# Attention and an FFN in one kernel: the first K in two loads, V of the first head group earlier, and the sums of the first batch loosened from its value passes

## The chip, the cores and the metric

The kernel runs on one core of one Trainium2 chip. The metric is the device time of one execution in microseconds (us); the median of several runs is compared. A difference is stated against the kernel before on the same chip.

Five engines work side by side, each through its own instructions in order: TensorE (PE in the profile; its weight loads are PEld), VectorE (DVE), ScalarE (ACT), GpSimd (POOL, which here only issues the loads) and SyncE (SP, which issues the stores). They wait for each other by semaphores.

## The reference, cut to what matters

```python
def _attn_ref(q, k, v):                     # each (8, 12, 448, 64): batch, heads, tokens, dim
    scale = 1.0 / np.sqrt(q.shape[-1])
    scores = scale * np.matmul(q, k.transpose(0, 1, 3, 2))
    scores = scores - np.max(scores, axis=-1, keepdims=True)
    attn = np.exp(scores)
    attn = attn / (np.sum(attn, axis=-1, keepdims=True) + 1e-09)
    return np.matmul(attn, v)

def _moe_ref(x, w_in, w_out):               # x (3584, 768), w_in (768, 2048), w_out (2048, 768)
    h = x @ w_in
    g = h * (1.0 / (1.0 + np.exp(-h)))
    return g @ w_out
```

The heads of a token are laid side by side (12 x 64 = 768) between the two. Inputs and the output are float32.

## The kernel before, in words

**Data.** Loads convert to float16 on the way. A *head group* is four of the twelve heads of a batch, so a batch has three groups. In a group's tile for K or Q, partition 32h + i holds head h and the fourteen tokens 14i to 14i + 13. VectorE transposes it in 32x32 blocks, so that the head dimension comes onto partitions: `turn_k` (line 371) and `turn_q` (line 392). Since two float16 values are moved as one float32, a score is made of two products (even and odd dims, `e` in `score`, line 398). The key tokens of K are put in four chunks `c` of up to 128 keys: token `first + c` of each of four sets `x` (`X_TOK`, line 234). For the first group ("lone") the sets begin at tokens 0, 4, 8 and 12, and the last has two tokens only, so that chunks 0 and 1 have 128 keys and chunks 2 and 3 have 96 (`KROWS`).

**Stages.** For each group: scores (line 403), exponentials from PSUM into SBUF (`expo`, line 434), the sums of the exponentials by a product with ones (`attend`, part 0; line 494 for batch 0, line 480 for pairs of groups later), two value passes (`attend`, parts 1 and 2; line 465), and the division: `inverse` (line 533) turns the sums (539), inverts them (556) and spreads the inverses over the tokens (560), and `norm` (line 593) multiplies. Then the FFN: the first product (609), tanh (625) and gate (650), and the second product, in plain form for the first 256 rows (`plain`, line 830; line 832) and with seven products in place of eight for the rest (line 820). The last four batches make the first product in the same manner (line 740).

Batch 0 is cut into two pieces of queries (seven and seven token sets), so its three groups make six *units*, numbered 0 to 5: units 0 to 2 are the first queries of groups 0 to 2, units 3 to 5 the second. In batch 0 two chunks of scores lie in one burst (`per_burst`). Units 0 to 3 (`TILED = 4`) write scores into three pairs of PSUM banks (`s_ring`), while sums and values share two banks (`m_ring`).

**The order.** Nothing is ordered at run time. A planner (`Order`, line 96, and the loop at line 1735) plays the kernel through with estimated times, and writes each engine's instructions in the order in which it started them. Its constants (such as `DMA_ROW`, `NEAR`, `HOLD`, `SHY`) are estimates and preferences; they cost nothing on the chip, but change the order. An operation starts in the plan when `when(deps)` has passed: a dependency is an operation, or a pair of it and a slack which is taken off its end. VectorE and ScalarE take the ready operation with the lowest time plus `bias`.

- `Order.load` (157) prices a load by rows and bytes. The POOL queue issues loads in the order of their planning (lines 946 to 982): K and Q of groups 0, 1, 2, then V of the whole batch in four loads, then further Q, w_in in four quarters of three loads, K and Q of batch 1, w_out in four quarters, V of batch 1 between its second and third quarter, then batch by batch.
- `qk_at` and `run_qk` start scores, `av_at` (1598) and `run_av` start sums and value passes. These stand in one list, `av_seq`: sums, values 1, values 2 of unit 0, then of unit 1, and so on. Only its first is looked at.
- `after_sums` (1673) plans the three steps of the inverse. The first waits for the inverse of the unit before (`inv_op[-1:]`), the last also for the last four norms (`norm_op[-4:]`), since the spread inverses of all units lie in the same place, `R[:, 0]`.
- `moe` is the list of FFN work, from which `moe_ready` (1438) takes the first that is ready. `queue_ffn1` (1018) puts in the first product, whose `deps` name the w_in loads; `queue_plain` (1268) puts in the plain second product, in steps of four with the w_out loads.
- Where PE would wait before the first FFN product, `run_zeros` (1719) multiplies zeros into an idle bank. The first stretch of it has `FIRST` blocks of 128 columns.

Of the kernel before, what the change touches and what calls it, by code (L numbers as in the profile page):

```python
# [9 lines left out]
FP16 = mybir.dt.float16  # L10
# [9 lines left out]
DMA_ROW = 0.022  # L20
DMA_RATE = 13400.0
DMA_SLOW = 13
DMA_GAP = 1.1
# [72 lines left out]
class Order:  # L96
# [60 lines left out]
    def load(self, rows, row_bytes, emit, ring=None, gate=None):  # L157
        op = Op("POOL", 0.58, emit)
        self.loads += 1
        row = DMA_ROW if self.loads <= DMA_SLOW else 0.004  # L160
        took = rows * (row + row_bytes / DMA_RATE) / 16 + DMA_GAP * (self.loads == 3)
        self.pool.append((op, took, ring, gate))
        return op
# [50 lines left out]
def kernel(  # L214
# [14 lines left out]
    HG = 4  # L229
# [21 lines left out]
    NEAR = 0.05  # L251
    LATE = -1.0
    COLD, FIRST = 8.5, 47
# [5 lines left out]
    COPY_B = -1  # L259
# [3 lines left out]
    HOLD = 0.4  # L263
    TILED = 4
    QUART = 1
    TURN = 4
    LOOK = 1
# [3 lines left out]
    SHY = 0.8  # L271
    TWB = 4
    SXB = 8
    PIECES = ((0, 7), (7, TPP))
# [36 lines left out]
    sT_t, inv_t, q_tile = {}, {}, {}  # L311
# [5 lines left out]
    def load_k(b, hg):  # L317
        t = sb.tile([128, TPP * D], FP16, name=f"rk_{b}_{hg}", tag="rk", bufs=NRK)
        nc.gpsimd.dma_start(out=t, in_=group_of(k, b, hg))
        rawk[(b, hg)] = t  # L320
# [50 lines left out]
    def turn_k(b, hg):  # L371
        t = rawk[(b, hg)][:].bitcast(FP32).rearrange("p (g i) -> p g i", i=32)
        kt = sb.tile([128, NCH, 4, 32, 2], FP16, name=f"KT_{b}_{hg}", tag="KT", bufs=3)
        KT[(b, hg)] = kt
        pairs = kt.rearrange("p c x i e -> p (c x i e)").bitcast(FP32)
        pairs = pairs.rearrange("p (c x i) -> p x c i", c=NCH, x=4)
        toks = X_TOK[form(b, hg)]
        x = 0
# [154 lines left out]
    def inverse(ns, step):  # L533
# [23 lines left out]
        else:  # L557
            for i, n in enumerate(ns):
                rdn_t[n] = R[:, i, 0 : g1 - g0]
            nc.vector.transpose(  # L560
                out=R[:, 0 : len(ns), 0 : g1 - g0],
# [355 lines left out]

    def plan_q(n):
# [15 lines left out]
    def plan_w_in(f0, f1):  # L934
        made = [
            od.load(256, 2 * (f1 - f0), lambda c=c: load_w_in(c, f0, f1))
# [10 lines left out]
    for hg in range(NG):  # L947
        plan_k(0, hg)
        plan_q(hg)
    plan_v(0, 0, NG)  # L950
# [33 lines left out]
    turned = {"n": 0}  # L984
# [30 lines left out]
    inv_op, norm_op = [], []  # L1015
    quads = []

    def queue_ffn1(b, g0, g1):
# [6 lines left out]
        for fs in turns:  # L1025
# [41 lines left out]
            def deps(fs=fs):  # L1067
                made = [(x_op[(b, cc, g0)], cc * mm(t1 - t0)) for cc in range(NDC)]
                made += [x for f in fs for x in ld_win[f]]
# [198 lines left out]
    def queue_plain(t, j):  # L1268
# [8 lines left out]
        def queue(f0, f1):  # L1277
# [16 lines left out]
            def deps():  # L1294
                if len(parts) < f0 // NPL:
                    return [None]
                made = [ld_wout[i] for i in range(len(ld_wout)) if wout_rows[i] < f1]
# [183 lines left out]
    def qk_at():  # L1481
# [10 lines left out]
        at = when([kt_op.get(units[n][:2]) for n in ns] + [qt_op.get(n) for n in ns])  # L1492
# [7 lines left out]
    def run_qk():  # L1500
# [4 lines left out]
        if n < TILED:  # L1505
            tiles = dict(zip(ys, s_ring.take(len(ys))))
# [91 lines left out]
    def av_at():  # L1598
        if not av_seq:
            return None  # L1600
        ns, part = av_seq[0]
# [71 lines left out]
    def after_sums(ns, op, nq, bank):  # L1673
        folds = per_burst(ns[0])
        last = norm_op[-4:]
# [156 lines left out]
```

## Time and profile before

| what | us | where from |
|---|---|---|
| median of three runs (388.13 to 388.76) | 388.36 | runs |
| profiled execution | 388.74 | run |
| its span, first to last instruction | 386.9 | page |
| first K issued, landed | 1.24, 4.87 | POOL timeline, time to landing |
| first Q landed | 5.40 | the same |
| second K and Q landed | 7.91, 8.50 | the same |
| third K and Q landed | 9.63, 10.22 | the same |
| V of batch 0 landed, four loads | 11.19, 12.19, 13.24, 13.77 | the same |
| w_in quarters landed | 18.43, 23.63, 29.76, 33.48 | the same |
| w_out quarters landed | 39.53, 43.62, 56.25, 60.06 | the same |
| first score on PE | 5.95 | PE timeline |
| first exponential | 6.56 | ACT timeline |
| first value pass | 16.00 | PE timeline |
| first FFN product | 24.70 | PE timeline |
| end of the last product | 383.1 | PE timeline |

All times count from the start of the span. A landing is the time of issue and the time to landing of that issue. In a row of the profile, `E<-P` names what is written and what is read, then the shape; in brackets stands how long the engine was idle before it, and what ended that.

### The profile page before, as it was taken

What the parts mean: (1) busy time and instruction counts of PE and PEld (TensorE: products, weight loads), DVE (VectorE), ACT (ScalarE), POOL (GpSimd) and SP (SyncE); (2) the same over time, 40 slices, a digit from 0 to 9 for tenths busy, and PEclk for the clock granted to TensorE, in tenths of its full rate; (3) what the DMA queues carried; (4) which work ended last, traced back from release to release, by engine and by line L of the source; (5) the groups of instructions that cost most, each with busy time, mean ns of one, the idle gap of its engine ahead of it and who ended that gap; (6) DMA issues with size and microseconds to landing.
All of it is one profiled execution on the core that took longest, in us unless ns stands there. A gap on an engine that the chain in (4) does not pass through costs nothing.

```text
span 386.9 us, 9007 instructions
## 1 busy us (share of the span) xinstructions
PE 378.5 (98%) x3569; PEld 191.1 (49%) x3569; DVE 297.5 (77%) x549; ACT 245.1 (63%) x381; POOL 87.9 (23%) x159
## 2 busy tenths in 40 slices
PE   8999998999999999999999999999999999999996
PEld 4567753443344444344434345555556655555653
DVE  2477676988988888898878879978887747777662
ACT  4979885798977677887568885316772038872000
POOL 7663453604224516060325000000000000000000
PEclk9999999999999999999999999999999999999999
DMA  7999999933719586483595200131001340001333
GB/s 113 200 206 208 179 167 210 164 60 35 110 31 180 88 154 87 59 108 59 105 167 72 43 2 20 29 87 31 0 2 41 100 107 0 2 0 44 102 93 92
DMA packets 37210, 34.41 MB, mean 89 GB/s; under 512 B 11696, under 2 KB 37168, under 8 KB 37168
## 3 DMA queue, kind: packets, MB, share of 16 engines
q0 software_dynamic: 26416, 22.82, 39.9%
q1 hardware_dynamic: 9984, 10.24, 9.7%
q10 hardware_dynamic: 768, 0.79, 0.8%
q8 instruction: 28, 0.46, 0.5%
q14 instruction: 14, 0.11, 0.1%
HBM read 45.61 MB, written 11.01 MB: 146 GB/s over the span
## 4 chain that ended last, share of the span: by engine, by line
PE 86%; DMA 9%; DVE 1%; POOL 1%; issue 1%; ACT 0%; ACTq 0%; DVEq 0%; POOLq 0%
PE P L820 29%; PE P L740 16%; PE P L609 16%; PE P L403 9%; PE P L465 9%; DMA rq<-in_q_dram 4%; DMA w_out_t<-in_moe_w_out_dram 3%; PE P L832 2%; DMA rk<-in_k_dram 2%; PE P L480 2%; PE P L1721 1%; POOL V L349 1%; PE P L494 1%; DVE ost L872 0%; DMA out_dram<-ost 0%
## 5 line engine op out<-in xcount | busy, mean ns | idle before, releaser
L439 ACT ACTIVATE E<-P 128x448 f16<-128x448 f32 (+4 forms) x172 | 151.9, 918 | 45.1 <-PE P L403 44.1
L609 PE MATMUL P<-xT,w_in_t 128*128 128x448 f16 (+1 forms) x480 | 81.4, 316 | 0.0
L349 POOL DMA_DIRECT2D V<-in_v_dram x84 | 46.0, 566 | 94.6 <-PE P L465 68.5
L609 PEld LDWEIGHTS <-w_in_t 128*128 128x128 f16 x480 | 43.0, 98 | 36.8 <-issue 16.0
L820 PEld LDWEIGHTS <-G 128*128 128x128 f16 x400 | 38.1, 98 | 29.3 <-issue 5.0
L403 PE MATMUL P<-rq,KT 32*128 32x448 f16 (+4 forms) x864 | 50.4, 340 | 0.4 <-ACT E L439 0.3
L650 DVE SCALAR_TENSOR_TENSOR G<-G,P 128x448 f16<-128x448 f16 x64 | 38.5, 609 | 13.3 <-ACT G L625 12.6
L820 PEld LDWEIGHTS <-S 128*128 128x128 f16 x312 | 29.6, 98 | 24.1 <-issue 4.9
L820 PE MATMUL P<-w_out_t,S 128*128 128x384 f16 x208 | 39.1, 326 | 0.7 <-DVE ost L872 0.7
L820 PE MATMUL P<-D,G 128*128 128x384 f16 x208 | 38.9, 326 | 0.0
L597 DVE SCALAR_TENSOR_TENSOR xT<-P,R 128x448 f16<-128x448 f32 (+1 forms) x54 | 28.4, 565 | 11.9 <-PE P L465 10.6
L625 ACT ACTIVATE G<-P 128x448 f16<-128x448 f32 x64 | 34.5, 545 | 3.4 <-PE P L609 2.7
L872 DVE TENSOR_TENSOR ost<-P,u 128x384 f32<-128x384 f32 x39 | 21.6, 554 | 18.2 <-PE P L820 13.9
L820 PE MATMUL P<-w_out_t,G 128*128 128x384 f16 x192 | 34.9, 326 | 0.0
L465 PE MATMUL P<-E,V 128*32 128x448 f16 (+2 forms) x672 | 34.3, 355 | 0.0
L740 PE MATMUL P<-sx,tw 128*128 128x448 f16 x144 | 30.2, 352 | 0.0
L740 PEld LDWEIGHTS <-tw 128*128 128x128 f16 x192 | 18.8, 98 | 17.5
L403 PEld LDWEIGHTS <-KT 32*128 32x128 f16 (+2 forms) x864 | 14.2, 98 | 26.4 <-issue 24.3
L879 ACT COPY ost<-P 128x384 f32<-128x384 f32 x13 | 6.3, 484 | 32.8 <-PE P L820 27.5
L384 DVE STREAM_TRANSPOSE KT<-rk 128x256 f32<-128x256 f32 (+3 forms) x48 | 16.6, 385 | 10.1 <-DMA rk<-in_k_dram 10.1
L465 PEld LDWEIGHTS <-V 128*32 128x32 f16 (+2 forms) x672 | 13.8, 95 | 20.0 <-issue 13.2
L450 DVE TENSOR_TENSOR T<-T,E 128x1792 f16<-128x1792 f16 x20 | 21.6, 1081 | 0.1
(78 smaller groups left out, 447.2 us busy)
## 6 DMA issues: line engine op xcount, KB each, us to landing
out_dram<-ost SPq DMA_DIRECT2D x208, 48.0 KB, 1.6
rk<-in_k_dram POOLq DMA_DIRECT2D x24, 224.0 KB, 5.4
rq<-in_q_dram POOLq DMA_DIRECT2D x21, 224.0 KB, 5.8
w_in_t<-in_moe_w_in_dram POOLq DMA_DIRECT2D x12, 256.0 KB, 8.4
w_out_t<-in_moe_w_out_dram POOLq DMA_DIRECT2D x4, 768.0 KB, 11.5
V<-in_v_dram POOLq DMA_DIRECT2D x43, 64.0 KB, 4.0
V<-in_v_dram POOLq DMA_DIRECT2D x40, 48.0 KB, 4.1
out_dram<-ost ACTq DMA_DIRECT2D x16, 48.0 KB, 1.8
```

The lines of the kernel that those rows point to most:

```text
L349: nc.gpsimd.dma_start(out=VT[(b, hg0)][32 * x : 32 * (x + 1), :, 0:count, :], in_=v[b, hs].rearrange("h (i g) d -> i h g d", g=TPP)[:, :, ...
L403: nc.tensor.matmul(out=P[p0 : p0 + 32 * (x1 - x0), pS[h], at : at + nq], lhsT=KT[(b, hg)][32 * h : 32 * (h + 1), c, x0:x1, :, e], rhs=QT[n ...
L439: nc.scalar.activation(out=E[(n, w)][0:kr, h0:h1, 0:nk], in_=P[0:kr, bank : bank + h1 - h0, 0:nk], func=AF.Exp, scale=attn_scale,)
L450: nc.vector.tensor_tensor(out=T[n], in0=T[n] if step else E[(n, 0)], in1=E[(n, step + 1)], op=ALU.add,)
L465: nc.tensor.matmul(out=a[32 * h : 32 * (h + 1), 0:nq], lhsT=w, rhs=e[k0:k1, h, at : at + nq], start=start, stop=stop, skip_group_check=True,)
L597: nc.vector.scalar_tensor_tensor(out=xc(b, cc)[:, 32 * g0 : 32 * g1], in0=acc[(n, part)][:, 0:nq], scalar=0.5, in1=rdn_t[n].rearrange("p g ...
L609: nc.tensor.matmul(out=h_t[(b, f, t0)][:, 0 : t1 - t0], lhsT=w_in_t[:, cc, 128 * f : 128 * (f + 1)], rhs=xc(b, cc)[:, t0:t1], start=(cc == 0),
L625: nc.scalar.activation(out=g, in_=h, func=AF.Tanh)
L650: nc.vector.scalar_tensor_tensor(out=g, in0=g, scalar=1.0, in1=h, op0=ALU.add, op1=ALU.mult)
L740: nc.tensor.matmul(out=pp_t[(*key, PBANK[m])], lhsT=w[:, c, :], rhs=xc(pb + x[0], 3 * x[1] + c) if isinstance(x, tuple) else sx_t[(pb, x)] ...
L820: nc.tensor.matmul(out=pr_t[(qd, BANK[m])][:, 0:OH], lhsT=w[:, f, :], rhs=W_[m][:, f, :], start=(f == 0 and BANK[m] == m), stop=(f == HF - 1),
L872: nc.vector.tensor_tensor(out=out, in0=a, in1=b, op=op)
```

## The change

Four things, and a number of the planner's constants:

- The first K comes in two loads, and the first Q ahead of both (`plan_first`). Part 0 has the token pairs 0, 2, 4 and 6 (eight tokens), which are chunks 0 and 1; part 1 the pairs 1, 3 and 5, which are chunks 2 and 3. Each part has its own turn, and the scores of chunk 0 ask only for the first.
- V of batch 0 comes in two sets of four loads: group 0 alone, ahead of K and Q of group 2 (`VFIRST = 2`), and groups 1 and 2 after them.
- In batch 0 the spread inverses get a buffer of four slots, `rdn_0`, in one of the two T buffers. The spreading waits for the norms of the unit that had the slot before, four units back. `av_at` may take the next sums of batch 0 ahead of the first in the list if that isn't ready.
- Prices of loads are changed (`DMA_ROW`, `DMA_GAPS`), w_out loads count as landed 1.3 us later (`SURE`) and w_in loads 0.39 us later, and `NEAR`, `FIRST`, `COPY_B`, `HOLD`, `LOOK` and `SHY` have other values.

```diff
-DMA_ROW = 0.022
+DMA_ROW = 0.004
-DMA_SLOW = 13
-DMA_GAP = 1.1
+DMA_GAPS = {1: 0.3, 3: 0.7, 4: 0.7}
...
-        row = DMA_ROW if self.loads <= DMA_SLOW else 0.004
-        took = rows * (row + row_bytes / DMA_RATE) / 16 + DMA_GAP * (self.loads == 3)
+        took = rows * (DMA_ROW + row_bytes / DMA_RATE) / 16 + DMA_GAPS.get(self.loads, more)
...
-    NEAR = 0.05
+    NEAR = 0.25
-    COLD, FIRST = 8.5, 47
+    COLD = 8.5
+    FIRST = 41
-    COPY_B = -1
+    COPY_B = -4
-    HOLD = 0.4
+    HOLD = 0.2
+    VFIRST = 2
-    LOOK = 1
+    LOOK = 2
-    SHY = 0.8
+    SHY = 1.0
+    SURE = -1.3
...
+    def load_k(b, hg, part=None):
+        if (b, hg) not in rawk:
+            rawk[(b, hg)] = sb.tile(
+                [128, TPP * D], FP16, name=f"rk_{b}_{hg}", tag="rk", bufs=NRK
+            )
+        t, src = rawk[(b, hg)], group_of(k, b, hg)
+        if part is not None:
+            t, src = token_pairs(t)[:, part::2], token_pairs(src)[:, part::2]
+        nc.gpsimd.dma_start(out=t, in_=src)
+
+    def token_pairs(t):
+        return t.rearrange("p (y e) -> p y e", y=TPP // 2)
...
+        if part is not None:
+            t = t.rearrange("p (y c) i -> p y c i", c=2)[:, part::2]
+            nc.vector.transpose(
+                out=pairs[:, 0 : 4 - part, 2 * part : 2 * part + 2], in_=t
+            )
+            return
...
+            homes = R[:, 0 : len(ns), 0 : g1 - g0]
+            if per_burst(ns[0]) == 2:
+                if "t" not in rdn_0:
+                    rdn_0["t"] = sb.tile([128, HG, S], FP16, name="rdn_0", tag="T", bufs=NT_)
+                at = ns[0] % HG
+                homes = rdn_0["t"][:, at : at + 1, :].rearrange("p h s -> p (h s)").bitcast(FP32)
+                homes = homes.rearrange("p (n g i) -> p n g i", n=1, i=32)
             for i, n in enumerate(ns):
-                rdn_t[n] = R[:, i, 0 : g1 - g0]
+                rdn_t[n] = homes[:, i]
             nc.vector.transpose(
-                out=R[:, 0 : len(ns), 0 : g1 - g0],
+                out=homes,
...
+    def plan_first():
+        plan_q(0)
+        made = [
+            od.load(512 - 128 * i, 4 * D, lambda i=i: load_k(0, 0, i), None if i else rk_ring)
+            for i in range(2)
+        ]
+        kt_ring.take()
+        turns = [
+            Op("DVE", 0.155 + (8 - 2 * i) / 30.0, lambda i=i: turn_k(0, 0, i), [made[i]], TURN,
+               then=rk_ring.give if i else None)
+            for i in range(2)
+        ]
+        kt_first.append(turns[0])
+        kt_op[(0, 0)] = turns[1]
...
     for hg in range(NG):
+        if hg == VFIRST:
+            plan_v(0, 0, 1)
+        if hg == 0:
+            plan_first()
+            continue
         plan_k(0, hg)
         plan_q(hg)
-    plan_v(0, 0, NG)
+    plan_v(0, int(VFIRST < NG), NG)
...
-                made += [x for f in fs for x in ld_win[f]]
+                made += [(x, 0.3 * SURE) for f in fs for x in ld_win[f]]
...
-                made = [ld_wout[i] for i in range(len(ld_wout)) if wout_rows[i] < f1]
+                made = [(ld_wout[i], SURE) for i in range(len(ld_wout)) if wout_rows[i] < f1]
...
+        made = [kt_op.get(units[n][:2]) for n in ns] + [qt_op.get(n) for n in ns]
+        if n == 0 and c == 0:
+            made[0] = kt_first[0]
...
-            tiles = dict(zip(ys, s_ring.take(len(ys))))
+            tiles = s_ring.take(len(ys))
+            if qk_seq[0][0][0] >= TILED:
+                tiles.sort()
+            tiles = dict(zip(ys, tiles))
...
-        ns, part = av_seq[0]
+        at = part_at(*av_seq[0])
+        if units[av_seq[0][0][0]][0] or (at is not None and at <= od.now):
+            return at
+        for i, (ns, part) in enumerate(av_seq[:12]):
+            if i and part == 0 and units[ns[0]][0] == 0:
+                first = part_at(ns, part)
+                if first is not None and (at is None or first < at):
+                    at = first
+                    av_seq.insert(0, av_seq.pop(i))
+                break
+        return at
...
+        if folds == 2:
+            if not rdn_op:
+                t_ring.take()
+            last = norm_ops.get(ns[0] - HG, [])
```

## The prediction

> **What bounds the kernel now.** I read the page first, then the chain of waits, then the first 62 us by engine. The page's slices say that TensorE is the bound:
>
> ```profile
> PE 378.5 (98%) x3569; PEld 191.1 (49%) x3569; DVE 297.5 (77%) x549; ACT 245.1 (63%) x381; POOL 87.9 (23%) x159
> ...
> PE   8999998999999999999999999999999999999996
> ```
>
> But busy is not work: line 1721 multiplies zeros to keep the array going. The windows of that line alone (columns: stretch, length, PE busy and matmuls, PEld, clock, DMA share, GB/s):
>
> ```profile
> 0.00:6.00 6.00, 4.63 (x12) 1.60 (x12) 1.00 0.59 79
> 6.00:10.00 4.00, 1.89 (x10) 0.80 (x10) 1.00 1.14 172
> 10.00:16.00 6.00, 4.20 (x26) 1.94 (x25) 1.00 1.38 199
> 16.00:20.00 4.00, 0.41 (x3) 0.10 (x1) 1.00 1.25 203
> 20.00:25.00 5.00, 0.23 (x1) 0.10 (x1) 1.00 1.20 207
> ```
>
> That is 11.35 us. In the same 25 us all PE rows are busy 22.53 us (4.68+3.71+6.00+4.00+4.14), so only 11.2 of the first 25 us are work; 13.8 us are zeros or nothing. From the first FFN product at 24.70 to the end of the last at 383.1 its gaps are 1.36, 0.70 and 0.11 us (at 60.1, 198.3 and 286.3). A change to the start can win only there, and must then keep it.
>
> Who ends the waits in the start? The timeline, ACT and PE rows:
>
> ```profile
> 6.56 10.35 ACT L439 ACTIVATE E<-P 128x896 f16<-128x896 f32 x12 [4.54 <-PE P L403]
> 17.11 1.73 ACT L439 ACTIVATE E<-P 128x896 f16<-128x896 f32 x2 [0.21 <-PE P L403]
> 19.30 1.72 ACT L439 ACTIVATE E<-P 96x896 f16<-96x896 f32 x2 [0.46 <-PE P L403]
> 22.27 1.72 ACT L439 ACTIVATE E<-P 128x1344 f16<-128x1344 f32 x2 [1.25 <-PE P L403]
> 24.81 1.29 ACT L439 ACTIVATE E<-P 96x1344 f16<-96x1344 f32 x1 [0.81 <-PE P L403]
> ```
> ```profile
> 16.00 0.57 PE L465 MATMUL P<-E,G 128*32 128x224 f16 x16
> ...
> 23.88 0.35 PE L465 MATMUL P<-E,G 96*32 96x224 f16 x5 [0.86 <-issue]
> 24.16 0.61 PE L403 MATMUL P<-rq,KT 32*96 32x224 f16 x16
> 24.70 1.80 PE L609 MATMUL P<-xT,w_in_t 128*128 128x224 f16 x17
> ```
>
> Until 16.9 the exponentials run without a gap (12 in 10.35, 0.863 us each): ACT is the bound and PE fills. Then ACT begins to wait for scores, because the value passes of line 465, none before 16.00, come all at once with sums, norms and the scores. DVE is busy 4.79 of the 5 us from 20 to 25. The first FFN matmul is at 24.70.
>
> The last view is who PE waits for in the whole span:
>
> ```profile
> PE P L832 <- DMA w_out_t<-in_moe_w_out_dram: 1.4, 1, 1.4
> PE P L1721 <- DVE cols L294: 1.2, 1, 1.2
> PE P L465 <- issue: 0.9, 1, 0.9
> PE P L820 <- DVE ost L872: 0.7, 1, 0.7
> PE P L403 <- ACT E L439: 0.3, 1, 0.3
> ```
>
> The first row is at 58.74 to 60.10: the fourth quarter of w_out lands at 60.06 (issued 49.34, 10.72 to landing). It is a clock that does not depend on PE.
>
> **First K in two loads.** Before, K lands at 4.87 (224 KB), Q at 5.40 (336 KB together), two turns take 0.70, the Q turn 0.37, the first score is at 5.95. After, Q (112 KB) and eight of the K's fourteen tokens (128 KB) suffice: 240 KB. Between the two landings 112 KB took 0.53, so 240 KB are there at 4.95. The Q turn (0.37) lies before that. A turn of 256 elements takes 0.43 (its row in the first 62 us), and the first score followed the turn by 0.05: 5.43 or, with a semaphore's slack, 5.46. **Gain 0.49**; bounds 0.04 (it lands only at 5.40) and 0.6 (lands at 4.87). The eleven zero matmuls that FIRST = 41 leaves (one less at 0.43) end by then. Issuing costs one more POOL step, 0.57, before the second K; that load is queued anyway (issued 2.46, landed 7.91). The second turn (192 elements, 0.34) lies behind the first scores and their 0.86 us of exponential; if these came late, it would cost its 0.34.
>
> The K loads become 896 rows of 256 B in SBUF. The nearest row is the last V load of the first batch, 384 rows of 256 B, 96 KB: it landed 0.53 after the one ahead of it (13.77 against 13.24), 181 KB/us, against 192 KB in 1.05 us for 512 B rows. So 224 KB cost 1.24 instead of some 1.13 us: 0.1 later for all behind. I keep 0.1 to 0.3.
> By the Trainium skill (DMA: Bandwidth & Descriptors, "Why small descriptors are slow (HBM only)") a 256 B descriptor loses 3 of 11 bus cycles, which as an estimate would make it 0.34 us and the total 0.2 us worse; the V row is nearer to the smaller loss, and decides.
>
> **V of head group 0 ahead of the third K.** Four more issues (0.54 to 0.69 each), and 224 KB are moved ahead of K and Q of group 2. Landings in order of bytes, taken from the landings before: 896 KB at 9.63, so V of group 0 at 9.7; K of group 2 at 10.8 (was 9.63), Q at 11.4 (was 10.22), the rest of V at 13.9, where all of V was at 13.77. POOL: at each time eight loads are out (the eleventh was issued at 8.19, after the third landed at 7.91); with the smaller ones that is still over 500 KB, 2.6 us at 195 KB/us, against 2.2 us from issue to landing in an empty queue (V loads at 45.9 to 47), so the transfers don't run dry. Group 2 now has K and Q turned at 11.8 (0.70 and 0.37; the K turn is done before the Q lands). Its scores are wanted at 12.74 - 0.49 = 12.25. It fits by 0.4; if it failed, ACT would idle for the difference. The same holds of a value pass that PE meets before its V has landed: scores stand behind it in PE's order, and ACT waits for them. The planner counts V as 1.0 later than its own estimate, which covers it.
>
> **Sums and inverses.** The sums passes (8 matmuls, 0.40 apart from the next) no longer stand behind value passes, and each group's inverse has a slot of its own, so it need not wait for the norms of the group before. Before, sums of groups 1, 2, 3 run at 17.41, 19.59, 21.16; they can now run as soon as their exponentials end, at about 13 and 16.5. No instruction is added; the slots lie in one of the two T buffers, free since the first add into T is at 47.92 and the last norm of batch 0 at 34.62. The inverse chain (0.65+0.17+0.20+0.41) moves from DVE's full stretch at 20 to 25 into 10 to 16, where it is busy 41%.
>
> **The sum for the start.** Real work done at 24.70 is 10.9 us. After: exponentials of four groups end at 6.07 + 16 x 0.863 = 19.9 (before 21.02). By 19.1, when the first w_in quarter is due (landed 18.43, plus 0.1, plus the new 0.4 of caution), PE can have done scores of four groups (8 x 0.51), sums of three (1.2) and values of three (3.0): 8.3 us. From there 24 FFN matmuls (2.2 us) and group 3's values are at hand and PE is full: 10.9 is reached at 21.7. The 0.86 "issue" wait agrees as a limit: adding up the counts it stands before the 349th matmul (23.88), and the 221st was at 18.46, 5.4 us earlier; if 128 matmuls can't come faster than that, the 349th can be at about 10.9 + 10.8 = 21.7 at the soonest (the 93rd, at 11.26 before, by 10.9). So at most 3.0 us; every link without a gap. **I take 2.3 us** (it contains the 0.49), nearer to the upper bound, since ACT, PE and DVE each have free time in 13 to 20; bounds 0.5 (the early first score alone) and 3.3.
>
> **The w_out wait.** PE would be at its place by 56.4, and the fourth quarter lands at 60.1 to 60.4. The plain products are planned as in `queue_plain`, whose loads now count as 1.3 us later, so others go first. At hand are the first twelve steps of the second and third plain tile, which need three quarters (third landed 56.25): 24 x 0.163 = 3.9 us, and sums and values of the head pair (0.7 + 3.1, run at 62.14 to 68.5 before). Banks and the exponentials of the pair decide. Bounds: -2.3 (all given back) to +1.4 (also the old wait gone). **I take +0.4.** Batch 2's scores stay where they are (its Q lands at 62.20, turned 63.26, scores 63.58); PE has the FFN of batch 1 instead.
>
> **The other constants** (NEAR, HOLD, LOOK, SHY, COPY_B) change the written order up to 250 us. Past the w_out wait PE's gaps there are one of 0.7 us, which bounds the gain; the loss by the gaps that another order can open, two of that size: -1.5. I take -0.2.
>
> Sum: 2.3 + 0.4 - 0.2 = 2.5. The profiled execution was 388.74 in all (span 386.9 and 1.84 around it), the median 388.36; 2.5 off gives 386.2 and **385.9**. Its own range is 384.5 to 387.1.
>
> **Rivals.**
> 1. *w_out takes it all back.* The wait grows from 1.4 to 3.7 us and PE leaves it at 60.1 to 60.4 as before. For: the landing is fixed by a queue that runs from 1.24 on. Against: the 3.9 us of plain steps named. Time 388.4. Chance 0.13.
> 2. *Group 2 comes late*, by the four V issues and loads now ahead of its K: ACT idles 0.5 to 1 us, and values move less. Or the planner leaves the values late, so that the change hardly does what it says. Gain 1.0: 387.4. Chance 0.14.
> 3. *Slower: copies ahead of exponentials.* COPY_B from -1 to -4 lets the two PSUM copies of each of 13 quads (0.48 each, 12.5 us) go ahead of exponentials, on whose banks the scores wait; ACT is 74% busy from 100 to 150 and 76% from 150 to 200. PE waits only if nothing else is ready. To be slower than before by 0.2% it needs 3.3 us, a quarter of the 12.5. At a third, 4.1 us: 390.0. Against: PE had other work at nearly each such time. Chance 0.11.
>
> **Chances.** Forecast 0.62, rivals 0.13, 0.14, 0.11. A difference of 0.2% (0.78 us) is about what can be told from none. Faster: 0.62 + 0.09 of rival 2 + 0.03 of rival 1 = 0.74; same 0.05 + 0.07 = 0.12; slower 0.11 + 0.03 = 0.14. The range, with the upper bound of the start (3.3 + 1.4) below and rival 1 above, is 383.9 to 388.6.
>
> **What would show it.** First score at 5.4 to 5.6; first value pass at 10 to 12; zeros (line 1721) down from 11.35 to 7 to 9 us; first FFN matmul at 18.5 to 21; exponentials gapless to 20; the L832 wait under 1 us. It is wrong if the fourth w_out quarter still ends a wait of 2 us or more, or if new gaps of PE stand between 100 and 250.

## The result, and the profile after

The changed kernel is slower: 393.78 us median of four runs (392.41 to 396.09) against 388.56 (388.13 to 389.71) on the same chip. The ratio is given as 1.0119 with a 95% interval of [1.0075, 1.0162]; the quotient of the two medians alone is 1.0134. The profiled execution took 392.41, its span 390.6.

The page, busy time and the 40 slices (PEclk is the granted clock in tenths):

```profile
PE 379.4 (97%) x3561; PEld 190.7 (49%) x3561; DVE 298.0 (76%) x549; ACT 245.0 (63%) x381; POOL 90.9 (23%) x164
...
PE   6999997999999999999989999999999999999996
...
PEclk8799999999999999999999999999999999999999
```

TensorE is busy 0.9 us longer with eight instructions fewer, and its clock is below full in the first two slices, which it wasn't before. The zeros, the same windows as before (line 1721 has become 1802; columns: stretch, length, PE busy, PEld busy, clock, DMA share, GB/s):

```profile
0.00:6.00 6.00, 3.78 (x12) 1.43 (x12) 1.00 0.65 69
6.00:10.00 4.00, 0.73 (x2) 0.21 (x2) 0.67 1.17 158
10.00:16.00 6.00, 2.92 (x11) 1.02 (x12) 0.65 1.20 156
16.00:20.00 4.00, 1.60 (x10) 0.51 (x7) 1.00 1.12 166
20.00:25.00 5.00, 1.42 (x8) 0.65 (x8) 1.00 1.23 203
```

10.45 us of zeros where there were 11.35, so little is won; the clock is 0.67 and 0.65 where it was 1.00; and the loads move 156 and 166 GB/s from 10 to 20 us where they moved 199 and 203. The ACT timeline, and the PE rows that answer to the two of before:

```profile
7.65 3.39 ACT L456 ACTIVATE E<-P 128x896 f16<-128x896 f32 x4 [5.63 <-PE P L420]
12.53 1.73 ACT L456 ACTIVATE E<-P 128x896 f16<-128x896 f32 x2 [1.49 <-PE P L420]
15.31 10.13 ACT L456 ACTIVATE E<-P 96x896 f16<-96x896 f32 x11 [1.05 <-PE P L420]
```
```profile
6.98 0.69 PE L420 MATMUL P<-rq,KT 32*128 32x224 f16 x16 [2.00 <-DVE KT L391]
...
14.16 0.57 PE L482 MATMUL P<-E,G 128*32 128x224 f16 x16
...
24.04 1.32 PE L633 MATMUL P<-xT,w_in_t 128*128 128x224 f16 x12
```

The first exponential is 1.09 us later, ACT then waits twice for scores, the first value pass is 1.8 us sooner, and the first FFN product 0.7 us. Who PE waits for in the whole span:

```profile
PE P L420 <- DVE rq L412: 2.0, 1, 2.0
PE P L420 <- DVE KT L391: 2.0, 1, 2.0
PE P L1802 <- DVE cols L295: 1.2, 1, 1.2
PE P L844 <- DVE ost L896: 1.2, 1, 1.2
PE P L482 <- DVE G L674: 0.8, 1, 0.8
```

The wait for w_out's fourth quarter (1.4 us before) is gone. Two of 2.0 us have come: for the first K, and for a turned Q at 65.8, which is batch 2's.

**Loads**, each from its issue and its time to landing, us:

| | before | after |
|---|---|---|
| first Q | 5.40 | 4.25 |
| first K (its two parts after) | 4.87 | 5.53 and 6.37 |
| V of group 0 complete | 13.77 | 10.62 |
| third K, third Q | 9.63, 10.22 | 11.71, 12.34 |
| V of batch 0 complete | 13.77 | 15.49 |
| first, second w_in quarter | 18.43, 23.63 | 21.72, 26.69 |
| fourth w_out quarter | 60.06 | 62.91 |
| first K and Q of batch 2 | 61.15, 62.20 | 63.97, 65.09 |

**Work done.** To compare runs I count PE's products without the zeros, by their columns (those that fill only a 32-row or 32-column strip at a quarter), scaled so that 346.8 us are the whole. What a kernel has done at a time can then be set beside the kernel before:

| at, us | before | after | difference |
|---|---|---|---|
| 16 | 2.68 | 2.68 | 0 |
| 28 | 11.49 | 9.57 | -1.9 |
| 60 | 38.66 | 38.01 | -0.7 |
| 66 | 44.00 | 41.37 | -2.6 |
| 240 | 204.25 | 200.65 | -3.6 |

1.9 us are lost by 28, most of it is made good by 60 (the kernel before waits for w_out there), and 2 us are lost again at 60 to 66. The rest is lost in small pieces. The end is 3.7 us later.

### The profile page after: what moved, and what is told of

Same layout as the page of the kernel before. It is cut to its first block, busy times and chain, and to the rows that moved or that the text cites. A ratio compares the mean times of both kernels' runs of the same rounds, so it can differ in the third digit from the quotient of the medians.

```text
span 390.6 us, 8992 instructions
## 1 busy us (share of the span) xinstructions
PE 379.4 (97%) x3561; PEld 190.7 (49%) x3561; DVE 298.0 (76%) x549; ACT 245.0 (63%) x381; POOL 90.9 (23%) x164
## 4 chain that ended last, share of the span: by engine, by line
PE 85%; DMA 9%; POOL 2%; issue 1%; DVE 1%; ACT 1%; SPq 0%; DVEq 0%; POOLq 0%; ACTq 0%
PE P L844 29%; PE P L764 16%; PE P L633 15%; PE P L420 10%; PE P L482 9%; DMA rq<-in_q_dram 7%; DMA rk<-in_k_dram 2%; PE P L856 2%; PE P L497 2%; PE P L1802 2%; POOL V L358 1%; PE P L511 1%; ACT E L456 1%; DVE ost L896 0%; DMA out_dram<-ost 0%
## 5 line engine op out<-in xcount | busy, mean ns | idle before, releaser
L420 PE MATMUL P<-rq,KT 32*128 32x448 f16 (+4 forms) x864 | 51.8, 345 | 4.0 <-DVE rq L412 2.0
L621 DVE SCALAR_TENSOR_TENSOR xT<-P,R 128x448 f16<-128x448 f32 x42 | 24.3, 617 | 7.5 <-PE P L482 6.1
L482 PEld LDWEIGHTS <-V 128*32 128x32 f16 (+2 forms) x672 | 13.9, 95 | 20.2 <-issue 13.4
## 6 DMA issues: line engine op xcount, KB each, us to landing
w_out_t<-in_moe_w_out_dram POOLq DMA_DIRECT2D x4, 768.0 KB, 11.4
```

Source lines behind the costliest of these rows:

```text
L420: nc.tensor.matmul(out=P[p0 : p0 + 32 * (x1 - x0), pS[h], at : at + nq], lhsT=KT[(b, hg)][32 * h : 32 * (h + 1), c, x0:x1, :, e], rhs=QT[n ...
L482: nc.tensor.matmul(out=a[32 * h : 32 * (h + 1), 0:nq], lhsT=w, rhs=e[k0:k1, h, at : at + nq], start=start, stop=stop, skip_group_check=True,)
L621: nc.vector.scalar_tensor_tensor(out=xc(b, cc)[:, 32 * g0 : 32 * g1], in0=acc[(n, part)][:, 0:nq], scalar=0.5, in1=rdn_t[n].rearrange("p g ...
```

## The experiments

Ratios are against the kernel before on the same chip and occasion, where its median was 389.56 to 390.04; they stand with a 95% interval, and are not the quotients of the medians.

### One part of the change undone

**e1_one_k**: the changed kernel with the first K in one load, ahead of the first Q.

```diff
-DMA_GAPS = {1: 0.3, 3: 0.7, 4: 0.7}
+DMA_GAPS = {3: 1.1}
-    FIRST = 41
+    FIRST = 47
-        if hg == 0:
-            plan_first()
-            continue
```

> The K split undone alone (K of group 0 in one load ahead of its Q, FIRST 47, gap 1.1 at the third load as before); V first, sums and the other constants stay. Theory A (the split is the cause: the first turn waits for both parts, 6.37, PE idles 2.0 us and the array's clock falls; 256 B rows slow the queue): first score at 5.95, no wait of PE over 1 us in the first 25 us, zeros at full clock from 6 us, fourth w_out quarter lands near 60.1 to 61, Q of batch 2 by 63.2, time 385.5 to 388. Theory B (the eight small V loads with only eight loads outstanding make the queue late): fourth w_out quarter still at 62 to 63, PE still waits about 2 us for Q of batch 2, time 389.5 to 391.5.

394.29 us, 1.0112 [1.0082, 1.0143]. The loss stays without the split; I had named 385.5 to 388 and 389.5 to 391.5. Its fourth w_out quarter lands at 63.29, Q of batch 2 at 65.44.

**e2_two_tiles**: part 1 of the first K goes into a buffer of its own.

```diff
+        if part == 1:
+            rawk["part"] = sb.tile([128, HG, S], FP16, name="rk_part", tag="T", bufs=NT_)
```

> As the changed kernel, but part 1 of the first K is loaded into a buffer of its own, so that the first turn has nothing to wait for but part 0 (landed 5.53). Theory A: first turn at 5.55, first score at 6.05 instead of 6.98, PE's idle time before it 1.1 instead of 2.0 us, time 0.7 to 1.5 us below the changed kernel (392.0 to 393.0). Theory B: the first score moves as said, but the queue's lateness decides at the scores of batch 2, so the time stays within 0.5 us of the changed kernel (393.3 to 394.3).

394.37 us, 1.0119 [1.0088, 1.0151]: no gain. Its time doesn't price the false wait, though: the fourth w_out quarter lands at 65.38 in it, 2.5 us later than in the changed kernel, and PE waits 2.9 us for w_out. But the trace shows what the first turn waited for. DVE in the changed kernel, then in this one:

```profile
4.28 0.41 DVE L412 STREAM_TRANSPOSE rq<-rq 128x224 f32<-128x224 f32 x1 [2.55 <-DMA rq<-in_q_dram]
6.47 0.70 DVE L391 STREAM_TRANSPOSE KT<-rk 128x256 f32<-128x256 f32 x2 [1.79 <-DMA rk<-in_k_dram]
```
```profile
5.53 0.45 DVE L397 STREAM_TRANSPOSE KT<-rk 128x256 f32<-128x256 f32 x1 [0.86 <-DMA rk<-in_k_dram]
7.35 0.38 DVE L397 STREAM_TRANSPOSE KT<-rk_part 128x192 f32<-128x192 f32 x1 [1.37 <-DMA rk_part<-in_k_dram]
```

In the changed kernel both turns run together at 6.47, behind the landing of part 1 (6.37), although part 0 had landed at 5.53: the two parts lie interleaved in one tile, and the reader of one is made to wait for both. With a tile of its own the turn comes at 5.53, right after part 0's landing (5.51), and the first score at 6.04, where the unsplit K had it at 5.95. So even without the false wait the first score isn't sooner than with the K in one load.

**e3_warm**: the zeros are made 4608 columns longer on the chip, not in the plan, so that PE doesn't idle ahead of the first score.

```diff
-    op = Op("PE", n / rate, lambda n=n, at=zb: run_zeros(n, at))
+    more = 4608 if n == FIRST * 128 else 0
+    op = Op("PE", n / rate, lambda n=n + more, at=zb: run_zeros(n, at))
```

> As the changed kernel, but the first stretch of zeros is 4608 columns longer on the chip (not in the plan), so that it ends at about 6.9 where the first score can start at 6.98. If the fallen clock is what costs: granted clock 1.00, scores of the first two groups at 0.5 instead of 0.9 us per 16 matmuls, real work behind by 1.0 instead of 1.9 us at 28 us, time 392.5 to 393.2. If it only fills ACT-bound or load-bound time: clock 1.00, but time within 0.4 us of the changed kernel.

393.69 us, 1.0099 [1.0062, 1.0137]. Work done is 1.2 us ahead of the changed kernel at 14, 0.7 at 28, 0.8 at 60, and at 66 the lead is 0.2: batch 2's Q, landed at 64.82, takes it back; PE stands 2.01 us for it, its clock then falls to 0.55, and at 70 the run is 1.4 behind the changed kernel. The slow clock of the start is real, but with it gone the time is no better.

**e4_v_whole**: V of batch 0 in four loads behind the third Q, as before.

```diff
-    VFIRST = 2
+    VFIRST = 3
```

> As the changed kernel, but V of batch 0 in four loads behind the third K and Q (VFIRST 3). Theory B: the w_in quarters and w_out come back toward the kernel before (first w_in quarter by 19.5 instead of 21.7, fourth w_out quarter by 61 instead of 62.9), the wait for Q of batch 2 shrinks under 1 us, time 390 to 391.5. Theory A: first score still near 7.0, w_out within 0.7 us of the changed kernel, time 393 to 394.5.

391.04 us, 1.0028 [0.9994, 1.0062]. This gives most of it back. The fourth w_out quarter lands at 61.27 and Q of batch 2 at 63.45, 1.6 us sooner than in the changed kernel.

### One part alone, on the kernel before

**e5_sums**: the slots for the inverses and the choice of sums out of turn, nothing else.

```diff
         last = norm_op[-4:]
+        if folds == 2:
+            if not rdn_op:
+                t_ring.take()
+            last = norm_ops.get(ns[0] - HG, [])
```

> The kernel before with the change's third part alone: slots for the spread inverses of batch 0, and sums that may go ahead of value passes. Loads, prices and constants as before. If loosening the sums is worth what the prediction took it for, the sums of groups 1 and 2 run at about 13 and 16 instead of 17.4 and 19.6, first FFN product 0.5 to 1.5 us earlier, time 0.5 to 1.5 us below before unless the w_out wait (1.36 us before) grows by as much. If the value passes alone set the pace, less than 0.4 us either way. It has no part in the slowdown in either case.

391.03 us, 1.0051 [1.0011, 1.0091]. Work done is the same as before up to 60 us (11.49 at 28), so this part alone wins nothing at the start. At 66 it is 2.2 behind: the fourth w_out quarter, whose load isn't touched, landed at 61.09 in this execution, and PE stood 2.4 us for it. The ten times lie in two bunches, 389.2 to 391.1 and 392.8 to 394.1; why is not settled.

**e6_v8_behind** and **e8_v_first**: V in eight loads, all behind the third Q; and V of group 0 ahead of the third K, the rest behind.

```diff
-    plan_v(0, 0, NG)
+    plan_v(0, 0, 1)
+    plan_v(0, 1, NG)
```
```diff
+        if hg == 2:
+            plan_v(0, 0, 1)
         plan_k(0, hg)
...
-    plan_v(0, 0, NG)
+    plan_v(0, 1, NG)
```

> The kernel before with V of batch 0 in eight loads instead of four (group 0, then groups 1 and 2), all still behind the third K and Q: the count of loads without the new place. If the number of small loads with eight outstanding is what makes the queue slow, the first w_in quarter lands at 20 to 21 (18.43 before), the fourth w_out quarter at 61.5 to 63.5, time 1.5 to 4 us above before. If it is the place ahead of the third K, landings stay within 0.7 us of before, and the time within 1 us.

> The kernel before with V of group 0 ahead of the third K in four loads and the rest of V behind it, as in the change; nothing else. If this part is the cause of the slow queue: first w_in quarter at 20 to 21.5, fourth w_out quarter at 62 to 63.5, a wait for Q of batch 2, time 2 to 4 us above before. If the queue is slow only together with the other parts: landings within 0.7 us of before and the time within 1 us.

391.81 us, 1.0058 [1.0034, 1.0083], and 391.46, 1.0033 [1.0002, 1.0063]. The number of loads is enough, whatever their place: the fourth w_out quarter lands at 63.74 and 62.64, Q of batch 2 at 65.90 and 64.80. V of group 0 first does give work sooner (1 us ahead at 14), and the lead is gone at 28.

**e7_constants**: the planner's preferences and SURE alone, not the prices.

```diff
-    NEAR = 0.05
+    NEAR = 0.25
-    COPY_B = -1
+    COPY_B = -4
-    HOLD = 0.4
+    HOLD = 0.2
-    LOOK = 1
+    LOOK = 2
-    SHY = 0.8
+    SHY = 1.0
+    SURE = -1.3
```

> The kernel before with NEAR, HOLD, LOOK, SHY, COPY_B and SURE of the change, and nothing else: loads, their prices and FIRST as before. By what the changed kernel and the run with V whole showed at 60 us (no w_out wait left), the 1.36 us there go, and the time is 0.5 to 1.3 us below before, unless the Q of batch 2 (landed 62.2, turned 63.26) ends the next wait; then within 0.5. If COPY_B and the rest open new gaps later (the rival of the prediction), 0.5 to 3 us above before.

390.86 us, 1.0018 [0.9989, 1.0047]. The time is that of before within the interval. Its profiled execution was its slowest (394.07), and shows how a stop at batch 2's Q can be paid twice. Its PE wait, and its windows (last columns: clock, DMA share, GB/s):

```profile
64.58 0.94 PE L404 MATMUL P<-rq,KT 32*128 32x448 f16 x8 [2.01 <-DVE rq L396]
```
```profile
62.00:64.00 2.00, 0.57 (x4) 0.95 1.29 190
64.00:66.00 2.00, 1.42 (x10) 0.50 1.06 179
66.00:68.00 2.00, 2.00 (x19) 0.50 1.23 172
68.00:70.00 2.00, 2.00 (x28) 0.50 0.95 129
70.00:72.00 2.00, 2.00 (x28) 0.84 0.55 100
```

After 2.01 us without work the clock is at half for 6 us. In the changed kernel's profiled execution, 2.05 us at the same place left it at 1.00.

**e11_k_split**: the split of K alone, with V in four loads, the old preferences, and a plan that knows that both turns wait for both parts.

```diff
-DMA_GAPS = {1: 0.3, 3: 0.7, 4: 0.7}
+DMA_GAPS = {1: 0.3, 2: 0.5, 3: 0.3, 4: 1.3}
-    VFIRST = 2
+    VFIRST = 3
...
-                [made[i]],
+                made,
```

> The first K in two loads alone, its Q ahead: V whole behind the third K, sums and constants as before. The plan is told what the profile showed (both turns wait for both parts; gaps as landed), and the zeros last until then (FIRST 59), so that the array does not idle. If the split costs by itself: first score at 6.8 to 7.1 (5.95 before), exponentials 1 us later through the start, fourth w_out quarter 0.5 to 1.5 us later, time 0.8 to 2 us above before, with the granted clock at 1.00. If it costs only through the fallen clock and the other parts: within 0.6 us of before.

393.73 us, 1.0083 [1.0043, 1.0123]. The fourth w_out quarter lands at 63.69 with V in four loads, and PE waits 2.3 us for it. That the split costs this by itself isn't shown, since the run keeps the new prices: its plan expects that quarter at 57.52. Up to 25 us its loads are only some 0.5 us late (second w_in quarter 24.96), and from 10 to 16 us they move 195 GB/s; e4, also with V in four loads, 194; e6 and e8, with eight, 143 and 149.

**e12_lead**: no load is changed. Five fills of an unused buffer stand on GpSimd between V's loads and the next Q's (one run).

```diff
+    def hold_pool():
+        t = sb.tile([128, HG, S], FP16, name="held", tag="T", bufs=NT_)
+        t = t.rearrange("p h s -> p (h s)").bitcast(FP32)
+        for _ in range(5):
+            nc.gpsimd.memset(t, 0.0)
```

> The kernel before with five fills of an unused buffer on GpSimd's engine between the four V loads of batch 0 and the next Q load: no load is added, split or moved, but the later ones are issued 2 to 5 us later, with less time between issue and transfer. If short notice is what makes the queue slow (as with eight V loads, where the first w_in quarter was issued at 11.3 to 13.4 and landed at 20.4 to 21.8), the w_in quarter lands 2 us or more after 18.43, with packets of over 0.3 us among its rows, though the queue never runs empty. If it is the number or size of the loads, the landings move only by what the queue ran empty.

395.8 us. POOL's timeline and two windows of it (clock, DMA share, GB/s last):

```profile
6.97 4.55 POOL L956 MEMSET held<- 128x896 f32 x5
11.47 0.57 POOL L329 DMA_DIRECT2D rq<-in_q_dram  x1
12.03 1.40 POOL L358 DMA_DIRECT2D w_in_t<-in_moe_w_in_dram  x2
```
```profile
10.00:16.00 6.00, 6.00 (x87) 1.00 1.20 154
16.00:20.00 4.00, 4.00 (x109) 1.00 1.10 168
```

The Q's issue is 3.3 us later than before (11.47 against 8.19), and the loads move 154 and 168 GB/s where they moved 199 and 203: nearly the changed kernel's 156 and 166. They slow down after the fills have ended, not during them (193 GB/s from 10 to 12 us, 148 and 122 in the next two stretches of 2 us). In the changed kernel the w_in loads are issued from 11.96, in the kernel before from 8.78. So loads that are issued late, with little queued ahead of them, move slower in this run, and not only later. First w_in quarter 20.52, fourth w_out quarter 63.55, Q of batch 2 65.69.

### What the plan believes

The planner's own bookkeeping gives the time at which it expects each load. Set beside the traces (a slack of the dependency, 0.39 for w_in and 1.3 for w_out, comes on top in the changed kernel):

| landing, us | plan before | trace before | plan after | trace after |
|---|---|---|---|---|
| first w_in quarter | 20.84 | 18.43 | 18.72 | 21.72 |
| fourth w_out quarter | 58.94 | 60.06 | 56.82 | 62.91 |
| first Q of batch 2 | 61.15 | 62.20 | 59.03 | 65.09 |

Before, the plan was 2.4 us too careful at w_in and 1.1 us too hopeful at the two others. The new prices (DMA_ROW 0.004 for the first loads too) expect all three 2.1 us sooner, while on the chip they land 3 us later: now the plan is 3.0, 6.1 and 6.1 us too hopeful.

The kernel before's trace is the earliest of six executions with its loads untouched (with e5, e7, and e9, e10 and e15 below): in these the three land at 18.43 to 19.31, 60.06 to 61.72 and 62.20 to 63.86. So 1 to 3 us of the lateness are the change's.

The planners of the other runs, set beside their traces, fit. At the fourth w_out quarter the plan is too hopeful by 8.6 us in e2, 7.3 in e1, 6.2 in e11, 5.9 in e3, 5.8 in e6, 4.7 in e8 and 4.4 in e4, which cost 0.3 to 1.2% (and by 4.6 in e12's one run); by 2.2 to 3.0 in e5, e7, e10 and e17, which cost 0 to 0.7%; and by no more than 1.0, or not at all, in e9, e13, e14, e15 and e16, which cost nothing.

**e9_wout_price**: the kernel before, with the third w_out quarter priced 1.9 us longer. No load changes. **e10_prices**: besides, the first loads at the times of the kernel before's trace. **e15_again**: e9 once more.

```diff
-        ld_wout.append(od.load(128 * (f1 - f0), 2 * DM, lambda: load_w_out(f0, f1)))
+        ld_wout.append(od.load(128 * (f1 - f0), 2 * DM, lambda: load_w_out(f0, f1), more=1.9 * (f0 == NFF // 2)))
```
```diff
-        took = rows * (row + row_bytes / DMA_RATE) / 16 + DMA_GAP * (self.loads == 3)
+        took = rows * (0.004 + row_bytes / DMA_RATE) / 16 + {1: 0.4, 3: 1.4}.get(self.loads, more)
```

> The kernel before with one number of the plan changed: the third w_out quarter is priced 1.9 us longer (it landed 5.7 us after the load ahead of it, and was priced 3.8), so that the plan also knows that all behind it, K and Q of batch 2 too, comes later. If the plan's price is what makes the 1.36 us wait, and other work is at hand: no wait for w_out above 0.3 us, no wait for Q of batch 2 above 0.5 us (in the run with SURE alone the wait moved there, 2.0 us), time 0.7 to 1.4 us below before. If the work at hand is used up by then, the wait comes back elsewhere and the time stays within 0.4 us.

> As the run before, and the loads of the start priced as they landed in the kernel before (0.004 per row for all, 0.4 us more at the first load and 1.4 at the third), so that the plan takes V of batch 0 as landed at 13.7 and not at 15.3. Loads themselves as in the kernel before. Value passes from 14.7 to 15 instead of 16.0, first FFN product 0.5 to 1.3 us earlier, real work ahead by 0.5 to 1 us at 28 us; time 0.5 to 1 us below the run with the w_out price alone if this is kept to the end, the same if batch 2's Q sets the pace.

> The kernel before with the third w_out quarter priced 1.9 us longer in the plan, once more, on another chip or at another time: if its gain is one of the order and not of that chip, 0.995 to 0.9995 with an interval below 1; if it was chance, an interval around 1.000.

e9: 389.31 us, 0.9971 [0.9943, 0.9998]; again, on another occasion: 388.99, 0.9970 [0.9947, 0.9992]. The wait for w_out is gone, and none has taken its place at 60 to 70 us in either profile. e9's list:

```profile
PE P L1721 <- DVE cols L294: 1.2, 1, 1.2
PE P L465 <- issue: 0.9, 1, 0.9
PE P L480 <- DVE G L650: 0.7, 1, 0.7
```

This is the version that beats both kernels, by 0.3%. Its lead in work done is 1.3 us at 60 and at 100, and it is given back between 120 and 150. Part of that is the wait for G in the list, 0.69 us at 143.96 (1.37 at 145.16 in e15): VectorE makes that G behind the turn of a K, for whose load it had waited 1.52 us. The rest isn't explained. e10 is level, and not below e9 as expected: 390.30, 1.0004 [0.9969, 1.0039]. Its prices also take the fourth w_out quarter in the plan from 60.84 to 58.23 (landed 61.16), and the wait for it is back with 1.8 us.

**e13_told**: the changed kernel, every load as it is, with a plan that is told the landings of the trace. **e14_told_warm**: the same with FIRST 49.

```diff
-DMA_GAPS = {1: 0.3, 3: 0.7, 4: 0.7}
+DMA_GAPS = {1: 0.3, 2: 0.5, 3: 0.3, 4: 1.1, 12: 0.5, 13: 0.4, 17: 2.2}
-    SURE = -1.3
+    SURE = 0.0
-                [made[i]],
+                made,
-        ld_wout.append(od.load(128 * (f1 - f0), 2 * DM, lambda: load_w_out(f0, f1)))
+        ld_wout.append(od.load(128 * (f1 - f0), 2 * DM, lambda: load_w_out(f0, f1), more=3.4 * (f0 == NFF // 2)))
```

> The changed kernel with every load as it is; the plan alone is told when they land: the first Q and the two parts of K at 4.27, 5.51 and 6.36 us (both parts before the first turn), the rest of V by 15.3, the first w_in quarter at 21.9 (it believed 18.7, the trace has 21.72), w_out's fourth quarter at 63.4 (believed 56.8, trace 62.91), Q of batch 2 at 65.6 (believed 59.0, trace 65.09); no caution (SURE 0). Theory A (the loss from 20 us on is a plan that expects the loads 3 to 6 us sooner than they land, and so puts work that waits ahead of work that could run): the waits for batch 2's Q and for w_out go below 0.7 us, and the time comes to 389 to 391, ratio 0.998 to 1.004. Theory B (the loads are late, and PE has no other work whatever the order): as the changed kernel, 392.5 to 394.5, ratio 1.008 to 1.013. Rival C (the lost 2 us of the start, the clock at half until 13 us, are the whole loss): real PE work is 1.9 us behind the kernel before at 28 us and stays so to the end, 391.5 to 392.5.

> The same with FIRST 49 in place of 41, so that the zeros last until about 5.8 us and the clock should not fall before the first scores. Theory A: real PE work some 1 us further at 14 to 28 us than without; the end 0.3 to 1 us sooner than there (388.5 to 390.5), as far as it isn't taken back at batch 2's Q near 66 us. Theory B: no better than the run that is warm but not told, 393 to 394. Rival C: the loss is gone, 388.5 to 389.5, and the one that is only told stays 2 us worse.

389.28 us, 0.9981 [0.9953, 1.0009], and 389.08, 0.9989 [0.9963, 1.0015]. The loss is gone in both, though the loads are as late as ever (e13: first w_in quarter 22.53, fourth w_out quarter 63.01, Q of batch 2 65.35). This refutes two other accounts: that late loads cost the time whatever the order, and that the loss of the start is the whole. Nor does the change win anything then: both intervals hold 1. e13's work done is 1.0 us behind the kernel before at 28 and level at 66 (44.16 against 44.00).

**e16_late_told** and **e17_early_told**: only the late landings told, from w_out's third quarter on; and only the early ones, up to the first w_in quarter.

```diff
-    SURE = -1.3
+    SURE = 0.0
...
+        ... more=6.3 * (f0 == NFF // 2)))
```
```diff
-DMA_GAPS = {1: 0.3, 3: 0.7, 4: 0.7}
+DMA_GAPS = {1: 0.3, 2: 0.5, 3: 0.3, 4: 1.1, 12: 0.5, 13: 0.4, 17: 2.2}
...
-                [made[i]],
+                made,
```

> The changed kernel, its loads and its start as they are; the plan is told only that w_out's third and fourth quarters and what follows land later: the fourth at 63.1, Q of batch 2 at 65.3 (it believed 56.8 and 59.0), no caution (SURE 0). It still believes in the first w_in quarter at 18.7 and starts the zeros and scores as before. If the untold late loads are where the 1.2% goes: PE no longer stops for batch 2's Q near 65 us (2.05 us in the changed kernel), real work at 70 within 1 us of that at 60 plus ten, and the time is 390.5 to 392, ratio 1.002 to 1.007: the loss of the start (1.9 us at 28) stays. If the start is the whole of it: 392.5 to 394.

> The complement: the plan is told the landings up to the first w_in quarter (21.9) and that the first turn waits for both parts of K; the late part keeps its own price and its caution of 1.3 us, so that it believes in w_out's fourth quarter at 60.0 and Q of batch 2 at 62.2, which should land near 63 and 65.4. If the late part decides: PE stops 1.5 to 3 us near 63 to 66, and the time is 391.5 to 393.5. If the early part decides: real work at 28 within 1.1 us of the kernel before, and 389 to 390.5 in the end, like the run that is told both.

e16: 389.80 us, 0.9986 [0.9960, 1.0013]. e17: 392.38 us, 1.0065 [1.0029, 1.0101]. The late belief decides: told alone it gives back all of the loss, the early one about half at most. I had expected e16 to keep the loss of the start, and it didn't: in its profile the start is even worse than the changed kernel's (the clock 0.57 from 10 to 16 us, work done 9.19 at 28, 2.3 behind), and still it has 42.78 at 66, 1.4 more than the changed kernel. PE near batch 2's Q, in the changed kernel and in e16:

```profile
62.95 0.81 PE L856 MATMUL P<-w_out_t,G 128*128 128x384 f16 x4
65.81 0.57 PE L420 MATMUL P<-rq,KT 32*128 32x448 f16 x8 [2.05 <-DVE rq L412]
66.32 0.82 PE L856 MATMUL P<-w_out_t,G 128*128 128x384 f16 x4
67.07 1.64 PE L482 MATMUL P<-E,V 128*32 128x448 f16 x32
```
```profile
63.66 1.47 PE L856 MATMUL P<-w_out_t,G 128*128 128x384 f16 x8
65.06 1.63 PE L482 MATMUL P<-E,V 128*32 128x448 f16 x32
66.62 2.12 PE L856 MATMUL P<-w_out_t,G 128*128 128x384 f16 x12
68.68 1.63 PE L482 MATMUL P<-E,V 64*32 64x448 f16 x32
```

The changed kernel writes batch 2's scores behind four plain products and ahead of value passes and further plain products, which could have run. Its Q landed at 65.09, was turned from 65.11 to 65.76, and all of PE stood until then. In e16 the same products and passes fill the time, and no score of batch 2 stands among them before 68.7. e17 stops at three places there instead, of which two are:

```profile
63.04 2.11 PE L856 MATMUL P<-w_out_t,G 128*128 128x384 f16 x12 [0.93 <-DMA w_out_t<-in_moe_w_out_dram]
66.00 0.57 PE L420 MATMUL P<-rq,KT 32*128 32x448 f16 x8 [0.85 <-DVE rq L412]
```

## Why the prediction was wrong

The forecast was 385.9, a gain of 2.5 us; the time was 393.78.

- **First K in two loads** (said: +0.49, bounds 0.04 to 0.6). Wrong in sign: the first score came at 6.98, 1.03 later. Two links failed. The false wait for part 1 wasn't thought of (e2 shows it: 0.9 us). And "240 KB are there at 4.95" was mis-sized: the rate of the stretch between the two landings doesn't hold for loads at the head of the queue. Part 0 came at 5.53, and at 5.22 to 5.93 in the nine runs with the split, while all 336 KB of an unsplit K and its Q are there at 5.29 to 5.71. The K's 224 KB took 2.12 us (first Q landed 4.25, part 1 6.37), where 1.24 were taken from a V load further back. That the 256 B rows are the cause isn't shown: the kernel before's next 224 KB, in long rows, took 2.51 (5.40 to 7.91). By the rule of the Trainium skill (DMA: Bandwidth & Descriptors, "Why small descriptors are slow (HBM only)") the rows cost 0.34 us as an estimate; no run here separates it.
- **V of group 0 first.** V at 9.7, third K and Q at 10.8 and 11.4, the rest at 13.9 were forecast; 10.62, 11.71, 12.34 and 15.49 came. The first three are 0.9 late, as the second K already is (8.81 against 7.91); the rest of V is 1.6 late, and the w_in behind it 2.6 to 3.2. "The transfers don't run dry" failed as a way of thinking: the queue has no stretch without a transfer in the trace, and yet it ran slower (156 GB/s), as e12 makes an untouched set of loads do when they are issued late.
- **Sums and inverses.** No work is added, as forecast, and alone they win nothing at the start (e5); e5's time is 0.5% longer, with the late w_out landing of its profile.
- **The sum for the start** (said: +2.3). It stood on a first w_in quarter at 18.5 to 19.1, which came at 21.72, on exponentials without a gap until 20, which had gaps of 1.49 and 1.05, and on a full clock. Measured -1.9 at 28. The first value pass at 14.16 missed the 10 to 12, the first FFN product at 24.04 the 18.5 to 21, and the zeros of 10.45 the 7 to 9. e14 and e16 show, though, that the start decides little: with the right plan the end is level with before from a start that is 0.7 to 2.3 us behind.
- **The w_out wait** (said: +0.4). The wait went, as forecast. The step that failed is this: "Batch 2's scores stay where they are (its Q lands at 62.20, turned 63.26, scores 63.58)", with the fourth quarter at 60.1 to 60.4. They landed at 65.09 and 62.91, and scores written for 59 stood in PE's order. I had named the caution of 1.3 us and not worked out the new prices beside it, which take 2.1 us off the same landings in the plan: the caution was undone before it began. That, with loads that came later, is what e16 gives back alone: 0.9986 against 1.0119. The prices aren't all of it: e17's plan expects w_out's fourth quarter at 60.02, later than the plan before (58.94), and with the loads later still it costs 0.65%.
- **The other constants** (-0.2): 1.0018 [0.9989, 1.0047] in e7 holds it. Its interval reaches to 1.8 us and so doesn't exclude the 1.6 us of rival 3, the copies ahead of exponentials; but e13, e14 and e16 keep COPY_B at -4 and are level with the kernel before. Rival 1 saw the place, a queue that doesn't depend on PE and takes the gain back, but priced it as if the queue kept its times. Rival 2 had the late third K, and its 0.5 to 1 us of idle ACT was 2.54 in two gaps; the most it took was a smaller gain.

So the loss is not of one part of the change. The parts make the loads 1 to 3 us later; prices changed in the same edit make the plan expect them 2.1 us sooner; and the order written from it costs the time.

## What to carry to other kernels

Where an order is fixed ahead from estimated landings, every change of the loads is a change of the order far behind it: set the plan's landings beside the trace's before anything else, and be late rather than early, since work put behind a load that the plan has too early stops all that stands behind it. (That a late plan is cheap is argued: no run here is late by more than 0.5 us at w_out.) Splitting a load to have its first half sooner needs a tile for each half, and here even the Q and the first half of the K were there no sooner than the whole of both had been (5.53 against 5.40). A lead at the start is worth only what the next fixed landing lets through.

## What the runs showed of the hardware

- Loads that GpSimd issues late moved slower, not only later: 154 GB/s from 10 to 16 us in e12 (one run) with nothing changed but the time of issue (3.3 us), 195 to 199 in six executions with these loads untouched. What it is inside the DMA stays open.
- Rows of 256 B in SBUF at the head of the queue: 128 KB in 1.28 us (first Q at 4.25, part 0 at 5.53), where 112 KB of the first Q took 0.53 before; but 224 KB in long rows took 2.51 just behind (5.40 to 7.91 before), so the rows need not be the reason.
- An idle stretch of PE of 2 us may or may not halve its clock: 2.00 us at the start of the changed kernel did (0.53 from 7 to 13 us), 2.05 us at 64 in the same execution didn't, 2.01 us in e7 did for 6 us, and 2.01 us in e3 did (0.55 from 66 to 68). The spread of the changed kernel's own runs goes with the mean clock: 392.41 at 0.990, 396.09 at 0.985.
